# Score runs at three more steps of a fused attention and feed-forward kernel

## The chip, the core and the metric

One core of one Trainium2 chip. The metric is the device time of one execution in microseconds (us). TensorE (PE) multiplies, VectorE (DVE), ScalarE (ACT) and GpSimd (POOL) work on tiles, SyncE (SP) issues most transfers; each engine works its own list in order.

## The reference, cut to what matters

```python
batch, n_heads, seq, head_dim = (4, 8, 768, 64)      # 16 clusters
q_assign = np.argmax(np.einsum('bhsd,hcd->bhsc', q_n, c_n), axis=-1)
k_assign = np.argmax(np.einsum('bhsd,hcd->bhsc', k_n, c_n), axis=-1)
mask = q_assign[:, :, :, None] == k_assign[:, :, None, :]
scores = np.where(mask, scale * np.matmul(q, k.transpose(0, 1, 3, 2)), -1000000000.0)
attn = np.exp(scores - np.max(scores, axis=-1, keepdims=True))
attn = attn / (np.sum(attn, axis=-1, keepdims=True) + 1e-09)
x = np.matmul(attn, v)                               # to (3072, 512)
...
h = x @ w_in                                         # (512, 2048)
return ((h - np.tanh(h)) @ w_out).astype(np.float32)
```

## The kernel before

The attention is cut into 96 **steps** `(n, half, s)`: `n` is one of 16 pairs of heads (four to a batch), `half` one half of its queries, `s` one third of its keys. A step makes scores (`begin`, PE line L544, tiles `sc`), takes their exponent (ACT, L566), keeps the pairs of equal cluster (`select`, four DVE instructions L576 that read `sc` and a `row` of cluster codes and write `e`; with these four the two `sc` tiles of the step are free), adds `e` up (POOL, L588 and L592) and multiplies with the values (`value`, PE L601, tiles `av`). There are buffers for the two `sc` tiles of one step and for the `e` of two steps: the scores of a step wait for the select of the step before, and a select waits for the `value` of two steps before. Steps 72 to 95 are the pairs 12 to 15.

While a batch's attention runs, the feed-forward part of the batch before it fills the rest of PE's time: up products (`pu`, L1012 and L1021) and then down products (`pd`, L1301), taken from a list `fill` in order; each has a weight, and step by step as many are taken as their share of the total weight asks. During steps 72 to 95 there are 56 up and 14 down products: the seven products `which` = 1, 2, 6, 7, 4, 5, 3 of Strassen's scheme, each for two blocks `j` = 0 and 1.

The scores contract over 64 rows (the trace's `64*128`), the values, and as a rule the products, over 128 (`128*64`): PE changes its shape on the way into and out of the scores. In a **run** (`runs(at)`) the scores of the next three steps are made in one piece, and the two groups of products between them are made in the `64*128` shape as well. A down product then fills two banks, which DVE adds with one instruction more. Runs stood at steps 50, 53, 56, 59, 62, 65, 68, 74, 77 and 80.

The third block of batch 2 is not multiplied in its turn but **set aside** (`set_aside`): for each of the seven products SP stores the left operand (`aside<-G`, 512 KB), DVE adds its two halves into a tile `u` (L1266), and SP stores that (`aside<-u`, 256 KB, L1269). There are two `u` tiles, so a third sum waits until the store of the first has landed. Such work collects in the list `behind` and is put into the program in the next step that neither is a run nor stands just in front of one:

```python
            if not run and not runs(at + 1):
                todo += behind
                behind.clear()
```

After step 95 the up products of batch 3 (`pu`) follow and then its down products, one level deeper (`pp`, L1519); the last group stores four quarter rows.

Of the kernel before, what the change touches and what calls it, by code (L numbers as in the profile page):

```python
# [58 lines left out]
def kernel(  # L59
# [10 lines left out]
    nc = tc.nc  # L70
# [13 lines left out]
    HCH = NCH // 2  # L84
# [95 lines left out]
    def fast():  # L180
# [275 lines left out]
        def summed(n: int, half: int):  # L456

            return n < HP and half == 0
# [204 lines left out]
        def joined(n: int):  # L663

            return n >= HP and not soon(n)
# [24 lines left out]
        def soon(n: int):  # L690
            return pairs[n][1] == HP - 1 or n == HP - 2
# [154 lines left out]
        HM = DM // 2  # L846
        HQ, HC = HF // 2, HM // 2
# [7 lines left out]
        SET_ASIDE = {  # L855
            (0, 0): 1, (0, 1): 5, (1, 0): 2, (1, 1): 4, (2, 0): 7, (3, 0): 6, (5, 0): 3
        }
        behind = []
        aside = dram.tile([len(ASIDE), 7, P, HF + HQ, P], F32, name="aside", bufs=1)

        def up_maker(q: int):
# [343 lines left out]
        def strassen_items(b: int):  # L1205
# [31 lines left out]
            aside_ = sum(block[0] == b for block in ASIDE)  # L1237

            def weight(i: int):

                return 4.55 if aside_ else 3.4

            def lower(j: int, which: int, part: int):

# [5 lines left out]
                else:  # L1250
                    nc.gpsimd.tensor_tensor(out=a12, in0=a12, in1=a11, op=ALU.subtract)

            def set_aside(which: int):

                d = [i for i in range(len(ASIDE)) if ASIDE[i][0] == b]
                for i in d:
                    c = slice(ASIDE[i][1] * P, (ASIDE[i][1] + 1) * P)
                    quarter_ = {
                        1: (0, 0), 2: (1, 0), 3: (1, 0), 4: (1, 1), 6: (0, 0), 7: (0, 1)
                    }.get(which)  # L1260
                    t = G[:, :, quarter_[0], quarter_[1], c] if quarter_ else left1[:, :, c]
                    nc.sync.dma_start(aside[i, SLOT[which], :, 0:HF], t)
                    total_ = late_pools["u"].tile([P, 2, TB], F32, name="u")
                    total_ = total_.rearrange("p a n -> p (a n)")[:, 0 : HQ * P]
                    total_ = total_.rearrange("p (a n) -> p a n", n=P)
                    nc.vector.tensor_tensor(  # L1266
                        out=total_, in0=t[:, 0:HQ], in1=t[:, HQ:HF], op=ALU.add
                    )
                    behind.append(lambda total_=total_, i=i: nc.sync.dma_start(  # L1269
                        aside[i, SLOT[which], :, HF : HF + HQ], total_  # L1270
                    ))

# [221 lines left out]
            def group(at: int):  # L1494
# [9 lines left out]
                quarters = m.rearrange("p (a n) -> p a n", n=HC)  # L1504
# [27 lines left out]
                def row(half: int, m_: int, j: int):  # L1532
                    return out_r[blocks[j][0], half * HCH + blocks[j][1]][:, m_ * HM : (m_ + 1) * HM]
# [24 lines left out]
                )  # L1558
                if final:
                    add(m, m, u0)  # L1560
                    nc.sync.dma_start(row(0, 1, 0)[:, 0:HC], quarters[:, 0])
                    nc.sync.dma_start(row(0, 1, 1)[:, HC:HM], quarters[:, 3])
                yield
                pair = bank()
                if final:
# [92 lines left out]
            if b == B - 1:  # L1658
                n = len(ups)
# [23 lines left out]
        NS = NCH // 2  # L1683
        HALF = HP * NS
# [161 lines left out]

        def runs(at: int):

            return 4 * HALF < at < 7 * HALF - 1 and at % NS == NS - 1 and at % (2 * HALF) < 2 * HALF - 1

        fill, whole, spent, since, over = [], 0.0, 0.0, 0, 1
        for at, (n, half, s) in enumerate(steps):
# [11 lines left out]
            now = []  # L1864
# [5 lines left out]

            run, chunks = runs(at), []
            if run:
                coming = now + fill
                for _ in range(NS - 1):
                    size = 1 if coming[0][1] == 2 else 3
                    assert all(len(it) == 4 for it in coming[:size]) or size == 1
                    chunks.append(coming[:size])
                    coming = coming[size:]  # L1880
                first_ones = sum(len(it) for it in chunks)
                while len(now) < first_ones + 1:
                    now.append(fill.pop(0))
                    spent += now[-1][0]
                now = now[first_ones:]
            elif runs(at + 1):
                ups_left = sum(len(it) == 4 for it in fill)
                if ups_left < 3 * (NS - 1):
                    for _ in range(ups_left % 3):
                        now.append(fill.pop(0))  # L1890
                        spent += now[-1][0]
            values_first = 1 in stages and not summed(n, half) or run
            if values_first:
                value(n, half, s)
            if 1 in stages:
# [9 lines left out]
                        spread(*to[:2])  # L1905
            if run:
                take(n, half)
                if half == 1 and joined(n):
                    total_both(n)
                for i, it in enumerate(chunks):  # L1910
                    to = steps[at + 1 + i]
# [83 lines left out]
            todo = []  # L1995
            if not run:
                todo, held = held, []
# [3 lines left out]
            if following and not run:  # L2001

                if half == 1 and s == NS - 1 and joined(n):
                    todo.insert(len(todo) - 1, lambda n=n: total_both(n))
            if LOAD in stages:
                stages[LOAD]()
            if TURN_Q in stages:
# [49 lines left out]
            if 2 * HALF <= at < 3 * HALF:  # L2057
                masks = 3 if half == 1 and s == NS - 1 else 2
                first_masks, todo = todo[:masks], todo[masks:]
# [238 lines left out]
    with ExitStack() as cx, tc.manual_schedule():  # L2298
        fast()
# [34 lines left out]
```

## Time and profile before

| what | value |
|---|---|
| median of 3 runs | 923.16 us (922.49 to 923.47) |
| profiled execution, its own time | 922.68 us |
| its span | 920.8 us |
| PE busy | 908.1 us |
| mean granted PE clock | 0.999 |

The span is from the first to the last instruction that the profiler saw; 1.9 us of the execution lie around it. "Busy" is time with at least one instruction in an engine.

### The profile page before, as it was taken

What the parts mean: (1) busy time and instruction counts of PE and PEld (TensorE: products, weight loads), DVE (VectorE), ACT (ScalarE), POOL (GpSimd) and SP (SyncE); (2) the same over time, 40 slices, a digit from 0 to 9 for tenths busy, and PEclk for the clock granted to TensorE, in tenths of its full rate; (3) what the DMA queues carried; (4) which work ended last, traced back from release to release, by engine and by line L of the source; (5) the groups of instructions that cost most, each with busy time, mean ns of one, the idle gap of its engine ahead of it and who ended that gap; (6) DMA issues with size and microseconds to landing.
All of it is one profiled execution on the core that took longest, in us unless ns stands there. A gap on an engine that the chain in (4) does not pass through costs nothing.

```text
span 920.8 us, 18740 instructions
## 1 busy us (share of the span) xinstructions
PE 908.1 (99%) x7286; PEld 498.5 (54%) x7286; DVE 692.9 (75%) x1280; ACT 295.2 (32%) x466; POOL 523.6 (57%) x403
## 2 busy tenths in 40 slices
PE   8999999999999999999999999999999999999997
PEld 4434433356653454445666664555455554449997
DVE  7779777887799598667477477767697587867995
ACT  5676653234333233333321121343231311221000
POOL 0236433467878565977765565787776866772000
PEclk9999999999999999999999999999999999999999
DMA  8777583794428985375584746566546745524532
GB/s 168 226 221 180 155 194 105 229 266 141 107 86 224 272 261 141 120 189 175 159 191 151 186 143 169 177 179 161 178 150 205 230 156 155 189 103 151 196 105 85
DMA packets 187439, 158.37 MB, mean 172 GB/s; under 512 B 119200, under 2 KB 161744, under 8 KB 184144
## 3 DMA queue, kind: packets, MB, share of 16 engines
q1 hardware_dynamic: 177696, 134.40, 51.9%
q0 software_dynamic: 6048, 20.98, 6.9%
q10 hardware_dynamic: 3600, 1.74, 0.7%
q8 instruction: 59, 0.97, 0.4%
q14 instruction: 36, 0.29, 0.1%
HBM read 130.33 MB, written 26.75 MB: 171 GB/s over the span
## 4 chain that ended last, share of the span: by engine, by line
PE 92%; DVE 4%; ACT 1%; issue 1%; DMA 1%; POOL 0%; SPq 0%; DVEq 0%; ACTq 0%
PE pu L1021 20%; PE sc L544 15%; PE av L601 14%; PE pd L1301 12%; PE pp L1519 9%; PE o L803 6%; PE pu L1012 5%; PE h L787 5%; PE hd L1152 3%; PE sim L405 1%; DVE e L576 1%; PE den L674 1%; PE den L647 1%; PE den L627 1%; POOL G L1215 0%
## 5 line engine op out<-in xcount | busy, mean ns | idle before, releaser
L592 POOL TENSOR_TENSOR sum<-sum,e 128x768 f32<-128x768 f32 x112 | 206.5, 1844 | 78.7 <-DVE e L576 73.9
L576 DVE SCALAR_TENSOR_TENSOR e<-row,code,sc 128x384 f32<-128x384 bf16 x336 | 184.0, 608 | 56.7 <-ACT sc L566 31.6
L566 ACT ACTIVATE sc<-sc 128x768 f32<-128x768 f32 x168 | 126.4, 793 | 203.0 <-PE sc L544 182.4
L544 PE MATMUL sc<-t,t 64*128 64x384 f32 x768 | 149.1, 505 | 1.6 <-DVE e L576 1.1
L601 PE MATMUL av<-e,vals 128*64 128x384 f32 x768 | 143.4, 495 | 0.0
L1021 PE MATMUL pu<-xT,w_in 128*64 128x384 f32 (+1 forms) x872 | 132.5, 441 | 0.2 <-DVE c L1317 0.2
L1215 POOL TENSOR_TENSOR G<-G,th 128x768 f32<-128x768 f32 (+1 forms) x51 | 88.1, 1745 | 58.1 <-ACT th L1213 58.0
L1301 PE MATMUL pd<-w_in,G 128*64 128x256 f32 (+1 forms) x960 | 108.8, 379 | 0.0
L544 PEld LDWEIGHTS sc<-t,t 64*128 64x128 f32 x768 | 67.8, 186 | 70.5 <-issue 32.7
L1021 PEld LDWEIGHTS pu<-xT,w_in 128*64 128x64 f32 x872 | 61.6, 137 | 62.2 <-issue 50.2
L1301 PEld LDWEIGHTS pd<-w_in,G 128*64 128x64 f32 (+1 forms) x960 | 74.0, 147 | 35.6 <-issue 6.3
L601 PEld LDWEIGHTS av<-e,vals 128*64 128x64 f32 x768 | 49.7, 136 | 77.3 <-issue 73.5
L588 POOL TENSOR_TENSOR sum<-e 128x768 f32<-128x768 f32 x28 | 52.4, 1872 | 60.4 <-DVE e L576 46.4
L1021 PE MATMUL pu<-diff,w_in 128*64 128x384 f32 x416 | 74.1, 488 | 0.5 <-DVE u L1006 0.4
L1213 ACT ACTIVATE th<-G 128x768 f32<-128x768 f32 (+1 forms) x51 | 39.5, 806 | 107.8 <-DVE G L1006 90.9
L803 PE MATMUL o<-w_out,g 128*64 128x512 f32 x256 | 57.4, 593 | 0.0
L1021 PEld LDWEIGHTS pu<-diff,w_in 128*64 128x64 f32 x416 | 29.3, 137 | 37.9 <-issue 31.5
L1006 DVE TENSOR_TENSOR G<-pu,u 128x384 f32<-128x384 f32 x72 | 38.8, 550 | 13.5 <-PE pu L1021 12.1
L1012 PE MATMUL pu<-diff,w_in 64*128 64x384 f32 x160 | 45.8, 482 | 0.0
L1012 PE MATMUL pu<-xT,w_in 64*128 64x384 f32 x152 | 45.1, 482 | 0.0
L787 PE MATMUL h<-xT,w_in 128*64 128x384 f32 x256 | 42.8, 486 | 0.0
L638 ACT COPY xT<-av 128x384 f32<-128x384 f32 x32 | 15.3, 480 | 82.1 <-PE av L601 82.0
(283 smaller groups left out, 1286.0 us busy)
## 6 DMA issues: line engine op xcount, KB each, us to landing
w_in<-up_factors SPq DMA_DIRECT2D x32, 896.0 KB
w_in<-down_factors SPq DMA_DIRECT2D x25, 1024.0 KB
again<-in_moe_w_in_dram SPq DMA_DIRECT2D x32, 256.0 KB
again<-in_moe_w_out_dram SPq DMA_DIRECT2D x32, 256.0 KB
vals<-in_v_dram SPq DMA_DIRECT2D x32, 192.0 KB
raw<-in_moe_w_in_dram POOLq DMA_DIRECT2D x12, 512.0 KB, 4.8
row<-q_codes SPq DMA_DIRECT2D x29, 192.0 KB
raw<-in_moe_w_out_dram POOLq DMA_DIRECT2D x10, 512.0 KB, 4.8
```

The source lines that it names most:

```text
L544: nc.tensor.matmul(sc[i][:, h, 0:TB], lhsT=turned[n, 1][r].rearrange("p a n -> p (a n)")[:, j * P : (j + 1) * P], rhs=turned[n, 0][r, half ...
L566: nc.scalar.activation(out=out, in_=sc[i][:, :, 0:TB], func=ACT.Exp, scale=SCALE)
L576: nc.vector.scalar_tensor_tensor(out=e[:, h].rearrange("p (j n) -> p j n", n=P), in0=rows[n, half][:, h], scalar=(codes[n][:, h, 1, j : j ...
L592: nc.gpsimd.tensor_tensor(out=s, in0=s, in1=pair[i], op=ALU.add)
L601: nc.tensor.matmul(avs[n, half][h * D : h * D + D], lhsT=vals[n][:, h, j], rhs=e[i][:, h], start=(j == 0), stop=(j == NCH - 1),)
L787: nc.tensor.matmul(h[r], lhsT=w_in[i][:, c, o * P : (o + 1) * P][:, r], rhs=xT[c][:, half], start=(c == 0), stop=(c == CD - 1),)
L803: nc.tensor.matmul(acc[sub][r], lhsT=gs[f % HF][:, f // HF, sub * P : (sub + 1) * P][:, r], rhs=w_out[f // FQ][:, f % FQ], start=(f == seq ...
L1012: return nc.tensor.matmul(ps, lhsT=streams[base + i][r, c, k_], rhs=right[c][r], start=start, stop=stop)
L1021: nc.tensor.matmul(ps[r], lhsT=streams[base + i][:, c, k_, r], rhs=right[c], start=(c == 0), stop=(c == CH - 1),)
L1215: nc.gpsimd.tensor_tensor(out=t, in0=t, in1=th, op=ALU.subtract)
L1301: nc.tensor.matmul(out_, lhsT=w, rhs=x, start=(i == 0), stop=(i == HF - 1))
L1519: nc.tensor.matmul(ps[r], lhsT=left[:, i, r], rhs=right[i], start=(i == 0), stop=(i == HQ - 1),)
```

## The change

1. Runs also at steps 83, 86 and 89. At 86 and 89 (`before_`) one down product is put in front of `value`, and `total_both`, which sums the denominators, behind the run.
2. The weights of the 14 down products of batch 2 become a list, which sets in which step each stands.
3. The stores of the `u` tiles collect in `stores` and are issued at the next `set_aside`, or in the next piece of `behind`.
4. Two of the last four stores are issued by ACT in place of SP.

```diff
             def weight(i: int):
-                return 4.55 if aside_ else 3.4
+                if not aside_:
+                    return 3.4
+                i = i // HCH * (HCH - aside_) + i % HCH
+                return (3.4, 3.4, 8, 3.4, 3.4, 3.4, 14.2, 3.4, 3.4, 7, 7, 6, 2.7, 2.7)[i]
...
+            def store_sums():
+                while stores:
+                    stores.pop(0)()
+
             def set_aside(which: int):
+                store_sums()
+                behind.append(store_sums)
...
-                    behind.append(lambda total_=total_, i=i: nc.sync.dma_start(
+                    stores.append(lambda total_=total_, i=i: nc.sync.dma_start(
                         aside[i, SLOT[which], :, HF : HF + HQ], total_
                     ))
...
                 if final:
                     add(m, m, u0)
-                    nc.sync.dma_start(row(0, 1, 0)[:, 0:HC], quarters[:, 0])
-                    nc.sync.dma_start(row(0, 1, 1)[:, HC:HM], quarters[:, 3])
+                    nc.scalar.dma_start(row(0, 1, 0)[:, 0:HC], quarters[:, 0])
+                    nc.scalar.dma_start(row(0, 1, 1)[:, HC:HM], quarters[:, 3])
...
         def runs(at: int):
-            return 4 * HALF < at < 7 * HALF - 1 and at % NS == NS - 1 and at % (2 * HALF) < 2 * HALF - 1
+            return 4 * HALF < at < 8 * HALF - 4 and at % NS == NS - 1 and at % (2 * HALF) < 2 * HALF - 1
...
-            run, chunks = runs(at), []
+            run, chunks, before_ = runs(at), [], False
             if run:
                 coming = now + fill
+                before_ = at > 7 * HALF
+                if before_:
+                    first_, coming = coming[0], coming[1:]
...
-                first_ones = sum(len(it) for it in chunks)
-                while len(now) < first_ones + 1:
+                first_ones = sum(len(it) for it in chunks) + before_
+                while len(now) < first_ones + (not before_):
...
+            if before_:
+                first_[2](lambda: None)
             if values_first:
                 value(n, half, s)
...
-                if half == 1 and joined(n):
+                if half == 1 and joined(n) and not before_:
                     total_both(n)
...
+            if before_ and half == 1 and joined(n):
+                todo.append(lambda n=n: total_both(n))
```

PE, before, from the scores of step 87 to the product behind the values of step 89 (a row without a step's number: each `sc` is one step, each `av x4` the values of the step before it):

```order
L544 MATMUL sc<-t_5265,t_5249 128x384 x4
L601 MATMUL av<-e,vals 64x384 x4
L1301 MATMUL pd<-w_in_136,G 64x256 x16
L544 MATMUL sc<-t_5265,t_5249 128x384 x4
L601 MATMUL av<-e,vals 64x384 x4
L1301 MATMUL pd<-w_in_136,G 64x256 x16
L544 MATMUL sc<-t_5265,t_5249 128x384 x4
L601 MATMUL av<-e,vals 64x384 x4
L1301 MATMUL pd<-w_in_138,G 64x256 x16
L544 MATMUL sc<-t_5686,t_5678 128x384 x4
```

PE now, from the scores of step 87 to the product in the middle of the run at step 89 (L1310 is the old L1301; `128x256` are products in the shape of the scores):

```order
L544 MATMUL sc<-t_5276,t_5258 128x384 x4
L1310 MATMUL pd<-w_in_138,G 128x256 x16
L544 MATMUL sc<-t_5276,t_5258 128x384 x4
L1310 MATMUL pd<-w_in_138,G 128x256 x16
L544 MATMUL sc<-t_5276,t_5258 128x384 x4
L601 MATMUL av<-e,vals 64x384 x8
L1310 MATMUL pd<-w_in_137,G 64x256 x16
L601 MATMUL av<-e,vals 64x384 x4
L544 MATMUL sc<-t_5743,t_5719 128x384 x4
L1310 MATMUL pd<-w_in_137,G 128x256 x16
L544 MATMUL sc<-t_5743,t_5719 128x384 x4
```

The scores of steps 87, 88 and 89 and then of 90, 91 and 92 now stand in one piece each, and the values of 87 and 88 stand together.

DVE, before, from the second half of the select of step 88 to that of step 89: one sum for the block set aside (L1266) lies between.

```order
L576 SCALAR_TENSOR_TENSOR e_6017<-row_5792,code_5492,sc_5990 128x384 [waits Activation_49]
L576 SCALAR_TENSOR_TENSOR e_6017<-row_5792,code_5492,sc_5990 128x384
L475 CAST listed_codes_73<-code_5914 128x12 [waits DVE_49]
L477 STREAM_TRANSPOSE qc_6025<-listed_codes_73 128x32 [waits DVE_49]
L1317 SCALAR_TENSOR_TENSOR c_6031<-pd_6000,w_in3_139 128x256 [waits DMASW7_49,PE_49]
L1266 TENSOR_TENSOR u_6037<-G_3124 128x512 [waits DMAHW7_49]
L1776 TENSOR_REDUCE largest_69<-again_5983 128x1 [waits DMAHW4_49]
L1776 TENSOR_REDUCE largest_69<-again_5985 128x1 [waits DMAHW5_49]
L576 SCALAR_TENSOR_TENSOR e_6073<-row_5792,code_5492,sc_6043 128x384 [waits Activation_49,Pool_49]
```

DVE now, from the second instruction behind the select of step 89 (the cast L475 is the first) to the beginning of that of step 90 (`DMAHWn` are eight counters that SP's transfers use in turn: 5 in front of the second sum is that of the store of `u_5904`, 7 in front of the third that of `u_6087`, 5 in front of the select that of the load of `row_6105`):

```order
L477 STREAM_TRANSPOSE qc_6081<-listed_codes_73 128x32 [waits DVE_49]
L1275 TENSOR_TENSOR u_6087<-G_3124 128x512 [waits DMAHW2_49]
L1275 TENSOR_TENSOR u_6091<-G_3124 128x512 [waits DMAHW5_49]
L1275 TENSOR_TENSOR u_6096<-G_3124 128x512 [waits DMAHW7_49,DVE_49]
L1785 TENSOR_REDUCE largest_69<-again_5831 128x1 [waits DMAHW3_49]
L1785 TENSOR_REDUCE largest_69<-again_5833 128x1
L749 TENSOR_TENSOR xT_5523<-xT_5523,den_5755 128x384 [waits DMAHW1_49,DMAHW0_49]
L749 TENSOR_TENSOR xT_5523<-xT_5523,den_6063 128x384 [waits DMAHW3_49,DMAHW2_49]
L1326 SCALAR_TENSOR_TENSOR w_in3_139<-pd_6114,w_in3_139 128x256 [waits PE_49]
L1785 TENSOR_REDUCE largest_69<-again_6101 128x1 [waits DMAHW3_49]
L1785 TENSOR_REDUCE largest_69<-again_6103 128x1 [waits DMAHW4_49]
L576 SCALAR_TENSOR_TENSOR e_6152<-row_6105,code_5951,sc_6138 128x384 [waits DMAHW5_49,Activation_49,Pool_49]
```

Three sums, of the products 2, 4 and 7, have come together in front of the select of step 90; before, the second and the third stood behind later selects.

SP's queue, before, behind the cast and the transposition (L1269 and L1262 store the sums and the left operands, `row_6041` is for the select of step 90):

```order
L479 DMA q_codes_6027<-qc_6025 4x32x32 [waits DMAHW6_49,DVE_49]
L1269 DMA aside_150<-u_5966 128x512 [waits DMAHW7_49]
L1269 DMA aside_150<-u_5969 128x512 [waits DMAHW0_49]
L1262 DMA aside_150<-G_3124 128x8x128 [waits DMAHW1_49]
L499 DMA row_6041<-q_codes_6027 128x768 [waits DMAHW6_49,DMAHW2_49]
```

SP's queue now, over the same stretch (L1278 and L1271 store the sums and the left operands, `again` are loads for the two reduces, `row` is the load that the select of step 90 needs):

```order
L479 DMA q_codes_6083<-qc_6081 4x32x32 [waits DMAHW4_49,DVE_49]
L1278 DMA aside_150<-u_5904 128x512 [waits DMAHW5_49]
L1271 DMA aside_150<-G_3124 128x8x128
L1278 DMA aside_150<-u_6087 128x512 [waits DMAHW7_49,DVE_49]
L1271 DMA aside_150<-G_3124 128x8x128 [waits DMAHW0_49]
L1278 DMA aside_150<-u_6091 128x512 [waits DMAHW1_49,DVE_49]
L1271 DMA aside_150<-G_3124 128x8x128 [waits DMAHW2_49,Pool_49]
L1773 DMA again_6101<-in_q_dram 128x384 [waits DMAHW3_49,DVE_49]
L1773 DMA again_6103<-in_q_dram 128x384 [waits DMAHW4_49,DVE_49]
L499 DMA row_6105<-q_codes_6083 128x768 [waits DMAHW5_49]
```

The load of `row_6105` stands behind the two loads of `again`, which wait for the two reduces on DVE, which stand behind the three sums. Before, the load of that row was issued between the first pair of stores and the sum of product 2.

## Rows read from the trace of the kernel before

**Rows 1.** The page, busy time of each engine.

```profile
PE 908.1 (99%) x7286; PEld 498.5 (54%) x7286; DVE 692.9 (75%) x1280; ACT 295.2 (32%) x466; POOL 523.6 (57%) x403
```

**Rows 2.** Timeline of PE (start us, us, what), scores of steps 87 and 88.

```profile
681.46 1.56 PE L544 MATMUL sc<-t,t 64*128 64x384 f32 x8
682.95 1.51 PE L601 MATMUL av<-e,vals 128*64 128x384 f32 x8
...
687.85 1.56 PE L544 MATMUL sc<-t,t 64*128 64x384 f32 x8
```

**Rows 3.** Timeline of PE, one run with down products.

```profile
523.03 1.56 PE L544 MATMUL sc<-t,t 64*128 64x384 f32 x8
524.43 3.62 PE L1301 MATMUL pd<-w_in,G 64*128 64x256 f32 x32
527.88 1.46 PE L544 MATMUL sc<-t,t 64*128 64x384 f32 x8
529.17 3.62 PE L1301 MATMUL pd<-w_in,S 64*128 64x256 f32 x32
...
534.01 3.67 PE L1301 MATMUL pd<-w_in,S 128*64 128x256 f32 x32
```

**Rows 4.** Timeline of PE, three places with waits.

```profile
670.06 0.92 PE L544 MATMUL sc<-t,t 64*128 64x384 f32 x4
...
672.17 1.51 PE L601 MATMUL av<-e,vals 128*64 128x384 f32 x8
...
695.72 1.51 PE L601 MATMUL av<-e,vals 128*64 128x384 f32 x8
...
701.45 1.97 PE L544 MATMUL sc<-t,t 64*128 64x384 f32 x8 [0.77 <-DVE e L576]
703.35 1.51 PE L601 MATMUL av<-e,vals 128*64 128x384 f32 x8
...
753.94 2.75 PE L1021 MATMUL pu<-xT,w_in 128*64 128x384 f32 x16
756.94 2.80 PE L1021 MATMUL pu<-xT,w_in 128*64 128x384 f32 x16 [0.25 <-DVE c L1317]
759.88 1.51 PE L1021 MATMUL pu<-diff,w_in 128*64 128x384 f32 x8
```

**Rows 5.** Timeline of DVE around the sum of product 2.

```profile
691.86 2.04 DVE L475 CAST listed_codes<-code 128x12 bf16<-128x12 f32 x1
...
697.05 2.28 DVE L1266 TENSOR_TENSOR u<-G 128x512 f32<-128x512 f32 x1 [2.28 <-DMA aside<-u]
...
700.18 2.17 DVE L576 SCALAR_TENSOR_TENSOR e<-row,code,sc 128x384 f32<-128x384 bf16 x4
```

**Rows 6.** Timeline of SP's queue (issues) over the same stretch.

```profile
694.80 0.93 SPq L1269 DMA_DIRECT2D aside<-u  x2
...
696.34 0.65 SPq L499 DMA_DIRECT2D row<-q_codes  x1
```

**Rows 7.** Windows of 1 us: each engine's busy time, PEclk, DMA share, GB/s.

```profile
696.00:697.00 1.00, 1.00 (x8) 0.43 (x6) 0.00 (x0) 0.74 (x2) 0.98 (x2) 1.00 1.03 342
```

**Rows 8.** Two DVE lines: ns of one, min/median/max.

```profile
L1266 DVE TENSOR_TENSOR u<-G x6: 684/1540/2284, 685.5 to 746.2; 128x512 f32<-128x512 f32 x6
...
L749 DVE TENSOR_TENSOR xT<-xT,den x10: 543/627/2174, 495.1 to 749.8; 128x384 f32<-128x384 f32 x10
```

**Rows 9.** DVE's waits, whole span: total us, times, longest.

```profile
DVE e L576 <- DMA row<-q_codes: 6.4, 4, 2.3
```

**Rows 10.** Timeline of SP's and ACT's queues, last stores.

```profile
914.04 0.33 SPq L1561 DMA_DIRECT2D out_dram<-again  x1
...
914.94 0.36 ACTq L1572 DMA_DIRECT2D out_dram<-again  x1
```

**Rows 11.** A window after the last matmul, columns as in rows 7.

```profile
919.50:920.00 0.50, 0.00 (x0) 0.00 (x0) 0.00 (x0) 0.00 (x0) 0.00 (x0) 0.81 0.04 16
```

More of the change, by code (lines that the diff above doesn't have):

```diff
@@ L857, in fast @@
         }
-        behind = []
+        behind, stores = [], []
         aside = dram.tile([len(ASIDE), 7, P, HF + HQ, P], F32, name="aside", bufs=1)
```

## The prediction

> **What bounds the kernel now.** I read the page first: PE is busy for 908.1 us [rows 1], so a change counts by what it takes from PE's own list or by a wait that it puts into it. Then the timeline of PE from step 84 on, for the gaps between starts; then DVE's and SP's timelines at the places where PE waited. The reader is to see three things. In [rows 2] a step outside a run costs PE 687.85 - 681.46 = 6.39 us. In [rows 3] the same work inside a run costs less: 529.17 - 527.88 = 1.29 for the scores, 527.88 - 524.43 = 3.45 for a product. And in [rows 4] PE three times starts late because DVE is late.
>
> **What the change takes away.** The order lists show the same matmuls, in part in another shape.
>
> *Changes of shape.* Scores, values (eight matmuls of 384 columns like the scores, so 1.29) and a product take 1.29 + 1.29 + 3.45 = 6.03; the 6.39 of [rows 2] hold 0.36 for going into the scores' shape and out. A run pays that once for three steps (0.21 of it is seen inside one: 534.01 - 523.03 = 10.98 [rows 3] against 3 x 1.29 + 2 x 3.45 = 10.77). Nine groups of scores become three, six round trips fewer: 6 x 0.36 = **-2.2**. In the other shape a down product needs one more DVE addition; [rows 3] show that PE loses nothing by it there.
>
> *Waits.* From the scores at 670.06 to the values 2.11 passed [rows 4], against 1.49 in [rows 2]: 0.62. From values to scores 701.45 - 695.72 = 5.73 against 4.90 in [rows 2], and from there to 703.35 1.90 against 1.49: 1.24 together. The two pairs of up products from 753.94 take 3.00 and 2.94 where four groups like the scores would take 2.58 each: 0.78. All three sit in steps 84 to 95 or just behind, where DVE's list is now another one; behind step 95 two down products now stand between the last denominators and the up products, before only one. I take all away: **-2.6**; the bounds are 0 and -2.6.
>
> **What it adds: the sums set aside.** This is the large term. Before, the sum of product 2 alone delayed a select: the cast began at 691.86, the sum at 697.05 (it had waited 2.28 for the store of an older `u`), and the select of step 89 started at 700.18 [rows 5]; the scores behind it lost the 1.24 above. Now the sums of products 2, 4 and 7 stand together between the selects of 89 and 90, with two `u` tiles, and the row for step 90 is loaded behind them. I follow it with zero at the scores of step 87.
>
> PE: the run's scores and two products take 10.98 [rows 3]; values of 87 until 12.3, of 88 until 13.6, a product until 17.1, values of 89 until 18.4, then 0.1 for the change of shape, scores of 90 until 19.8, product until 23.3. At **23.3** PE wants the scores of 91, which need the first half of the select of 90.
>
> DVE: the select of 89 needs the `e` that the values of 87 free, so it runs from 12.3 to 14.5 (2.17, [rows 5]). Cast, transposition, store of the codes and the store of the waiting `u` follow each other as in [rows 5], with the store issued at 694.80 [rows 6]: 2.94 from cast to issue, 5.19 until the buffer was free. So the store is issued at 17.4 and the second sum begins at 19.7; the first lies in the gap. A sum takes 0.68 to 2.28, median 1.54 [rows 8]: until 21.2. The third needs the store of the first, issued some 0.95 later (two issues, [rows 6]) and behind 512 KB: 17.4 + 0.95 + 2.25, and 1.5 for 512 KB at the 342 GB/s of [rows 7], is 22.1. It ends at 23.6. The two reduces take 0.9 (between the end of the sum and 700.18 in [rows 5]) until 24.5; only then can the second `again` be loaded and, 0.5 later, the row: issued at 25.0. In [rows 5, 6] the row was there 3.84 after its issue (696.34 to 700.18; no wait for it is seen): 28.8. The two scalings (0.63 each, at most 2.17 [rows 8]), one addition and two reduces fit in beside it. First half of the select, half of 2.17: 29.9. **PE waits 29.9 - 23.3 = 6.6.** The second tile comes later still, as at 701.45: +0.4.
>
> Bounds: with sums of 0.68, no time for the 512 KB and a row that lands in the 2.25 of a `u` store, the third sum ends at 21.3, the row is there at 24.9 and PE waits 2.7. With sums of 2.28 and a row load 2.3 later (the longest that a select has waited for one, [rows 9]) it is 24.4, 25.8, 31.9, 33.0: 9.7. I stay in the middle, since each link has a row of its own.
>
> A sum alone takes 0.68, yet the median is 1.54 and the one in [rows 5] took 2.28 while POOL was busy in almost every moment [rows 7]. The Trainium skill, "SBUF — State Buffer", section "SBUF: two separate sides", says that a DVE instruction with two SBUF inputs and a GpSimd instruction that reads SBUF lock each other out for a whole instruction. By that rule each of the three sums, with POOL adding `e` beside them, is a long one, and the wait would be nearer to 8 than to 6.6; the trace agrees with the rule for single sums.
>
> **Smaller terms.** The scores of step 93 now follow the values of 90 and 91 without a product between, and the select of 92 starts only with the end of the values of 90: its second half is over 2.2 after that, the scores ask for it after 1.29 + 0.1 + 0.65. With releases **+0.3** (0 to 1). The fourth of ACT's stores: before, SP's first left at 914.04 and ACT's last at 914.94 [rows 10]; four in one queue, 0.36 and a little each, put the last near 915.2, and all ends with its landing: **+0.25** (0 to 0.3). The first product in front of the values in steps 86 and 89 costs nothing: it is work that would stand elsewhere, and it covers the select that those values need. The denominators behind the run move two PE groups and four small transfers to a place where three steps pass before anyone needs them. The new weights move products, and with them the loads of their factors, which still have a product or more in hand.
>
> **Sum:** -2.2 - 2.6 + 6.6 + 0.4 + 0.3 + 0.25 = +2.75, on the profiled execution's own 922.68: 925.4. The median of the runs is 0.5 above that execution; I say **925.6 us**. Bounds of the long wait alone: 921.5 to 928.5.
>
> **Rivals.**
> - *PE does not wait for step 90* (the other side). Speaking for it: the first sum, and without locks all of DVE's own work between the selects (2.0 + 0.2 + 3 x 0.68 + 0.9 + 1.3 + 0.4 + 0.9 = 7.7), ends at 22.2, and stores might land faster than the one seen. Then only the gains are left: 922.68 - 2.2 - 2.6 + 0.55 = 918.4. It decides at a select of 90 that begins before 22.2. Against it: two transfers that DVE waits for in turn, each 2.25 in the only row there is.
> - *The clock falls during the wait.* The granted clock was still full until 919.5 and then fell [rows 11], some 5 us after the last matmul. If a wait of 6.6 lets it fall to 1.2 GHz, the next product takes twice 3.45: 925.6 + 3.5 = 929. No row shows a matmul at that clock, so the price may be smaller.
> - *The runs do not do what they are for:* outside the older runs the round trip costs nothing extra, or moves to the values, which now stand in pairs. Without the 2.2 it is 927.8. Against it: [rows 2, 3] show the same groups side by side.
>
> **How the numbers follow.** About 0.2% (1.85 us) is what a measurement of this kernel can tell from no change. Long wait as priced, 0.58 (0.30 of it over +1.85, 0.25 within, 0.03 faster); no wait, 0.22; clock falls, 0.15; runs without gain, 0.05. So faster 0.03 + 0.22 = 0.25, same 0.25, slower 0.30 + 0.15 + 0.05 = 0.50. The range, 920.0 to 930.0, takes in the bounds of the wait and the clock, and leaves out most of the case without a wait. The likeliest case's own range is 921.5 to 928.5.
>
> **What would show it.** Right: a gap of 3 to 10 us on PE in front of the second scores of the run at step 89, released by DVE's select; the third sum waiting for `aside<-u`, and the select of step 90 for `row<-q_codes`; three groups of scores with products of 3.45 between them in place of nine single ones. Wrong: scores of step 91 on time, or the three old waits still there. The prediction fails if the stores land within some 1.5 us of their issue, or if the select of step 89 ends well before 14.5.

## The result: 1.2% slower

| | kernel before | changed kernel |
|---|---|---|
| median, 6 runs each | 923.32 us (922.49 to 925.32) | 934.38 us (932.69 to 936.53) |
| ratio, 95% interval | | 1.012 (1.0103 to 1.0137) |
| profiled execution, its span | 922.68, 920.8 | 936.09, 934.2 |
| mean granted PE clock | 0.999 | 0.991 |

The time lies above the range of the prediction. I account for the two profiled executions, which differ by 13.4 us.

The page of the changed kernel, busy time; PE does the 7286 matmuls of [rows 1] in 2.6 us more, within a span 13.4 longer, so most of the difference is waiting:

```profile
PE 910.7 (97%) x7286; PEld 507.7 (54%) x7286; DVE 692.8 (74%) x1285; ACT 295.0 (32%) x466; POOL 524.0 (56%) x403
```

PE's timeline of the changed kernel, from the scores of step 87 to the first up products of batch 3:

```profile
690.40 1.56 PE L544 MATMUL sc<-t,t 64*128 64x384 f32 x8
...
701.38 2.80 PE L601 MATMUL av<-e,vals 128*64 128x384 f32 x16
...
708.85 1.56 PE L544 MATMUL sc<-t,t 64*128 64x384 f32 x8
710.25 2.11 PE L1310 MATMUL pd<-w_in,G 64*128 64x256 f32 x18
...
722.41 2.93 PE L544 MATMUL sc<-t,t 64*128 64x384 f32 x8 [8.55 <-DVE e L576]
725.11 4.51 PE L1310 MATMUL pd<-w_in,G 64*128 64x256 f32 x32
729.44 1.47 PE L544 MATMUL sc<-t,t 64*128 64x384 f32 x8
...
734.89 1.97 PE L544 MATMUL sc<-t,t 64*128 64x384 f32 x8 [0.48 <-DVE e L576]
736.79 1.51 PE L601 MATMUL av<-e,vals 128*64 128x384 f32 x8
738.13 3.62 PE L1310 MATMUL pd<-w_in,G 128*64 128x256 f32 x32
744.31 1.55 PE L647 MATMUL den<-sum,ones 128*64 128x384 f32 x4 [2.55 <-POOL sum L592]
745.78 2.31 PE L544 MATMUL sc<-t,t 64*128 64x384 f32 x8
748.03 1.51 PE L601 MATMUL av<-e,vals 128*64 128x384 f32 x8
...
760.97 0.87 PE L647 MATMUL den<-sum,ones 128*64 128x384 f32 x4 [0.30 <-POOL sum L592]
...
768.57 5.33 PE L1021 MATMUL pu<-xT,w_in 128*64 128x384 f32 x32
```

The run itself works: 701.38 - 690.40 = 10.98, to the hundredth the run of [rows 3], and from the scores of step 87 to those of step 90 pass 708.85 - 690.40 = 18.45, against 3 x 6.39 = 19.17 for three steps outside a run [rows 2]. Then come two waits. The scores of step 91 were wanted at 710.25 + 3.45 = 713.70 and start 8.71 later. The denominators of step 93 (L647) were wanted at 741.58 and start 2.73 later, released by POOL. Behind both, the same matmuls take longer: the scores at 722.41 need 2.70 to the next start, against 1.29 in [rows 3].

Windows of the changed kernel over these waits, columns as in [rows 7] (the number after the five engines is PEclk):

```profile
713.70:718.00 4.30, 0.17 (x2) 0.00 (x0) 2.43 (x6) 0.00 (x0) 0.00 (x0) 0.84 0.96 275
718.00:722.40 4.40, 0.00 (x0) 0.02 (x1) 1.52 (x4) 0.00 (x0) 0.00 (x0) 0.50 0.76 241
723.50:725.00 1.50, 1.50 (x6) 0.98 (x6) 0.57 (x2) 0.80 (x1) 0.00 (x0) 0.50 1.04 429
744.30:746.00 1.70, 1.69 (x6) 0.51 (x8) 0.00 (x0) 0.10 (x1) 1.70 (x2) 0.50 0.83 202
```

The clock fell to 0.50 (1.2 of 2.4 GHz) while PE waited and was still there when PE worked again.

DVE's timeline, the chain of the prediction:

```profile
706.34 2.25 DVE L1275 TENSOR_TENSOR u<-G 128x512 f32<-128x512 f32 x1
709.35 0.92 DVE L1275 TENSOR_TENSOR u<-G 128x512 f32<-128x512 f32 x1 [0.76 <-DMA aside<-u]
712.04 1.12 DVE L1275 TENSOR_TENSOR u<-G 128x512 f32<-128x512 f32 x1 [1.78 <-DMA aside<-u]
713.09 1.00 DVE L1785 TENSOR_REDUCE largest<-again 128x1 f32<-128x384 f32 x2
...
717.23 1.02 DVE L1785 TENSOR_REDUCE largest<-again 128x1 f32<-128x384 f32 x2 [1.87 <-DMA again<-in_q_dram]
721.13 2.19 DVE L576 SCALAR_TENSOR_TENSOR e<-row,code,sc 128x384 f32<-128x384 bf16 x4 [2.88 <-DMA row<-q_codes]
...
733.61 2.19 DVE L576 SCALAR_TENSOR_TENSOR e<-row,code,sc 128x384 f32<-128x384 bf16 x4 [3.02 <-POOL sum L588]
```

SP's queue:

```profile
715.27 0.44 SPq L499 DMA_DIRECT2D row<-q_codes  x1
```

POOL's timeline:

```profile
731.77 1.81 POOL L588 TENSOR_TENSOR sum<-e 128x768 f32<-128x768 f32 x1 [19.15 <-PE den L674]
```

The row was issued 24.87 after the scores of step 87 (predicted 25.0) and landed 5.86 later, when the select that waited for it started (predicted 3.84). The second wait was not in the prediction: POOL's sum of step 90 needs a `sum` tile. There are two, and until the denominators of pair 14 (L674, now behind the run, at 730.84) both hold that pair's sums. The select of step 90 was done at 723.3; POOL started at 731.77 and was late for everything after.

### The profile page after: what moved, and what is told of

Read it like the earlier page. It is cut to its first block, busy times and chain, and to the rows that moved or that the text cites. A ratio compares the mean times of both kernels' runs of the same rounds, so it can differ in the third digit from the quotient of the medians.

```text
span 934.2 us, 18747 instructions
## 1 busy us (share of the span) xinstructions
PE 910.7 (97%) x7286; PEld 507.7 (54%) x7286; DVE 692.8 (74%) x1285; ACT 295.0 (32%) x466; POOL 524.0 (56%) x403
## 4 chain that ended last, share of the span: by engine, by line
PE 83%; DVE 5%; DMA 5%; POOL 3%; issue 2%; ACT 1%; SPq 1%; ACTq 0%; DVEq 0%; POOLq 0%
PE pu L1021 20%; PE sc L544 12%; PE pd L1310 11%; PE av L601 11%; PE pp L1528 9%; PE pu L1012 6%; PE h L787 4%; PE hd L1152 3%; PE o L803 3%; DVE e L576 1%; DMA row<-q_codes 1%; PE sim L405 1%; POOL sum L592 1%; DMA hot<-q_codes 1%; DMA q_codes<-qc 1%
## 5 line engine op out<-in xcount | busy, mean ns | idle before, releaser
L1021 PE MATMUL pu<-xT,w_in 128*64 128x384 f32 (+1 forms) x864 | 130.3, 440 | 0.0
L1310 PE MATMUL pd<-w_in,G 128*64 128x256 f32 (+1 forms) x960 | 109.6, 381 | 0.0
L1310 PEld LDWEIGHTS pd<-w_in,G 128*64 128x64 f32 (+1 forms) x960 | 79.4, 157 | 31.4 <-issue 5.4
L1021 PE MATMUL pu<-diff,w_in 128*64 128x384 f32 x400 | 71.4, 488 | 0.4 <-DVE u L1006 0.4
L1012 PE MATMUL pu<-diff,w_in 64*128 64x384 f32 x176 | 49.6, 482 | 0.0
L1012 PE MATMUL pu<-xT,w_in 64*128 64x384 f32 x160 | 48.3, 482 | 0.0
```

Of the source, the lines that this page charges most:

```text
L1012: return nc.tensor.matmul(ps, lhsT=streams[base + i][r, c, k_], rhs=right[c][r], start=start, stop=stop)
L1021: nc.tensor.matmul(ps[r], lhsT=streams[base + i][:, c, k_, r], rhs=right[c], start=(c == 0), stop=(c == CH - 1),)
L1310: nc.tensor.matmul(out_, lhsT=w, rhs=x, start=(i == 0), stop=(i == HF - 1))
```

## Experiments

The names A, B, V, L, R, W are those of the expectations. Experiments 1 to 7 and 9 to 12 are edits of the changed kernel; 8 is one of the kernel before.

**1. Denominators in front of the run again.**

```diff
-                if half == 1 and joined(n) and not before_:
+                if half == 1 and joined(n):
                     total_both(n)
...
-            if before_ and half == 1 and joined(n):
-                todo.append(lambda n=n: total_both(n))
```

> The changed kernel with the denominators of pair 14 (L674) in front of the run of step 89 again; all else stays. Theory A (the denominators behind the run hold both `sum` tiles, so POOL's sum of step 90 starts 8 us late and its backlog makes PE wait again at 734.9, 744.3 and 761.0, with a low clock at 744 to 748): those three places, worth 0.59 + 0.41 + 2.73 + 0.72 + 0.76 + 0.47 = 5.7 us, are gone, POOL's L588 waits for `e` instead of for `den`, the long wait of 8.7 in front of the scores of step 91 stays: about 928.7. Rival B (POOL is late because the select of step 90 is late, whatever the tile): the second wait stays at 2 us or more and the time at 933 or more.

Measured: 930.28 us, ratio to before 1.0076 (1.0059 to 1.0092). POOL's waits from 700 to 740 (total, times, longest):

```profile
POOL sum L588 <- DVE e L576: 10.7, 1, 10.7
```

POOL now waits for `e`, the wait of 2.73 is gone, and 4.1 us with it. A holds, B falls. Not all that A lists belongs to the denominators: a wait of 0.34 in front of the last denominators stayed, and so did 0.68 at the scores of step 93 (0.27 late, 0.41 longer). The first wait is 7.7 because the denominators fill 0.78 of it.

**2. The row's load in front of the two loads of `again`.**

```diff
                 todo += behind
                 behind.clear()
+                if at == 7 * HALF + 3:
+                    todo.append(lambda: spread(n + 1, 0))
...
-                if to and to[2] == 0 and kind == known:
+                if to and to[2] == 0 and kind == known and at != 7 * HALF + 4:
```

> The changed kernel with the load of the row for step 90 issued right behind the three left operands and sums, in front of the two loads of `again`. Theory A (the row is late because its issue stands behind loads that wait for two reduces, which stand behind three sums): it is issued at about 711.6 in place of 715.27, the select of step 90 waits for DVE's own reduces and starts near 718.4 in place of 721.13, the wait in front of the scores of step 91 falls from 8.7 to about 6.0, the second wait stays: about 931.7. Rival B (the row lands when the stores of 512 KB are through, whenever it is issued): select at 721, no change, 934.4.

Measured: 935.57 us, ratio 1.0132 (1.0115 to 1.0149): nothing gained. SP's queue and DVE's timeline:

```profile
711.45 1.22 SPq L499 DMA_DIRECT2D row<-q_codes  x1
712.72 1.71 SPq L1773 DMA_DIRECT2D again<-in_q_dram  x2
```

```profile
719.17 1.05 DVE L1785 TENSOR_REDUCE largest<-again 128x1 f32<-128x384 f32 x2 [4.75 <-DMA again<-in_q_dram]
720.14 2.18 DVE L576 SCALAR_TENSOR_TENSOR e<-row,code,sc 128x384 f32<-128x384 bf16 x4
```

The row is issued early, but the select of step 90 now starts directly behind the two reduces, whose loads stand behind the row and landed at 719.2, over 6 us after their issue. A's number falls, the time is B's. When the row itself landed, this run does not show.

**3. Edits 1 and 2, and the reduces and loads of `again` of step 87 later.**

```diff
-                if not run and not runs(at + 1) and at != 7 * HALF:
+                if not run and not runs(at + 1) and at not in (7 * HALF, 7 * HALF + 3):
                     todo += [check_done, check_done, check_on, check_on]
```

> Both edits above, and the reduces and loads of `again` of step 87 moved to later steps. Theory A: the three sums end at 713.2, the select starts when the two additions and two older reduces are done or the row has landed, 716.6 to 717.5; the first wait is 3.4 to 4.3 in place of 8.7, the waits behind it are gone: 934.4 - 5.7 - 4.8 = about 923.9, or 921.6 if the clock no longer falls. Rival B (the place of the row and of the denominators are not the cause): above 930.

Measured: 931.15 us, ratio 1.0083 (1.0066 to 1.0100). The row is issued at 711.49; DVE has nothing else left and waits for it:

```profile
718.87 2.19 DVE L576 SCALAR_TENSOR_TENSOR e<-row,code,sc 128x384 f32<-128x384 bf16 x4 [4.40 <-DMA row<-q_codes]
```

7.4 us from issue to landing; and the last denominators wait 1.6 for POOL. So the place behind the reduces was not what made the row late. The time is that of rival B, though the denominators do cost something (experiment 1). Both 2 and 3 missed my numbers for one reason: I counted a fixed time from a load's issue to its landing, while SP's transfers of 706 to 712 were still on their way in front of it.

**4. Experiment 3, and the sum of product 7 behind the run.**

```diff
-            (0, 0): 1, (0, 1): 5, (1, 0): 2, (1, 1): 4, (2, 0): 7, (3, 0): 6, (5, 0): 3
+            (0, 0): 1, (0, 1): 5, (1, 0): 2, (1, 1): 4, (3, 1): 7, (3, 0): 6, (5, 0): 3
```

> The third kernel, and in it the sum of product 7 is collected two products later, so that it falls behind the run of step 89 and only the sums of products 2 and 4 stand in front of the select of step 90. Theory A (the chain of sums and stores is the rest of the wait): the sums end at 710.3, the select starts at 713.8 to 715.5, PE wants the scores of step 91 at 714.5 and waits 0.4 to 2.3; no second wait, no low clock: about 919, below the kernel before. Rival B (two sums behind the run make the next selects late instead): a wait of 2 to 4 us in front of the scores of step 93 or 94, about 922.

Measured: 930.94 us, ratio 1.0102 (1.0068 to 1.0136). With 0.75 MB less in front, the select of step 90 still waits for the row, issued at 710.06, until 717.08; PE's wait there is 3.8. A wait of 1.97 came up in front of the scores of step 94, where B had put one of 2 to 4. Both numbers are missed, and the sum itself was not the rest of the wait.

**5. The row in front of all stores.** Experiment 3, but the row right behind the codes; the older `u` stored before the run; product 7 later still (`(4, 1): 7`).

```diff
-            yield lambda: publish(n)
+            yield lambda: (publish(n), spread(n, 0) if n == len(pairs) - 1 else None)
...
                     first_, coming = coming[0], coming[1:]
+                    while stores:
+                        stores.pop(0)()
```

> The first kernel (denominators in front), and: the row for step 90 is loaded right behind the store of the codes, in front of all the stores for the block set aside; the store of the older `u` leaves before the run; the sum of product 7 is collected later; the reduces of step 87 come later. Theory V (volume: the row lands when the 2 to 3 MB of stores and loads that stand in the queue in front of it are through, at some 300 GB/s): with nothing in front it is issued near 709 and lands within 4 us, the select of step 90 starts by 713.5, PE wants the scores of step 91 at 714.5 and waits under 0.5: about 920.6. Theory L (latency: a row load takes its 6 to 7 us wherever it stands): the select starts at 715.5, the wait is about 2 and the clock falls behind it: about 924.

Measured: 927.35 us, ratio 1.0035 (1.0023 to 1.0046). DVE's and PE's timelines:

```profile
710.18 3.15 DVE L749 TENSOR_TENSOR xT<-xT,den 128x384 f32<-128x384 f32 x2
...
714.51 2.18 DVE L576 SCALAR_TENSOR_TENSOR e<-row,code,sc 128x384 f32<-128x384 bf16 x4
```

```profile
713.72 5.19 PE L1310 MATMUL pd<-w_in,G 64*128 64x256 f32 x29 [2.12 <-DVE w_in L1326]
```

The select no longer waits for the row, and the wait of 8 us is gone. When the row landed is not seen, only that it was there 6.1 after its issue at 708.41, so this run does not decide between V and L; experiment 10 does. Two other waits came up, and the time misses both numbers: a down product waits 2.12 for a PSUM bank that DVE frees only behind two additions (L749), and the last denominators wait 2.24 for POOL.

**6. Experiment 3 with the three left operands stored behind the run.**

```diff
-                    nc.sync.dma_start(aside[i, SLOT[which], :, 0:HF], t)
+                    keep_ = lambda i=i, t=t: nc.sync.dma_start(aside[i, SLOT[which], :, 0:HF], t)
+                    if which in (2, 4, 7):
+                        lefts_.append(keep_)
+                    else:
+                        keep_()
```

`lefts_` is issued with the first `behind` after step 89.

> The third kernel (denominators in front, row early, reduces later) with the stores of the three left operands, 512 KB each, moved behind the run; the three sums, their stores and the row's place stay. Theory V (volume): the row, issued near 711, lands within 4 us, the select of step 90 starts at 714.5 to 715 in place of 718.87 (shifted by at most 0.7 between executions), and the wait in front of the scores of step 91 falls from 6.4 to 1.5 to 2.5: about 925. Theory L (latency): the row lands 6 to 7 after its issue as in the third kernel, select at 717.5 or later, no gain, 931.

Measured: 932.67 us, ratio 1.0106 (1.0072 to 1.0141). The row, issued at 711.08, landed at 716.69, 5.6 later: between V and L. The first wait fell from 6.4 to 2.97, but the 1.5 MB, now in front of the load of `each` (the denominators, of which L714 takes the reciprocal), brought a new one of 5.45 in front of the scores of step 94.

**7. Without the run at step 89.**

```diff
-            return 4 * HALF < at < 8 * HALF - 4 and ...
+            return 4 * HALF < at < 7 * HALF + 4 and ...
```

> The changed kernel without the run at step 89; the runs at 83 and 86, the weights and the three sums together stay. Theory A (the three sums, the stores and the row load behind them are the first wait; the denominators behind the run the second): the first wait stays at 5 us or more, there is no second: 927 to 930. Rival R (the run at step 89, which asks for the scores of 91 after one product, is what makes the select late): no wait over 2 us in steps 90 and 91, and 923 or less.

Measured: 931.17 us, ratio 1.0079 (1.0060 to 1.0097). PE's timeline:

```profile
720.26 2.93 PE L544 MATMUL sc<-t,t 64*128 64x384 f32 x8 [8.03 <-DVE e L576]
```

The wait does not need the run at 89: what collects behind the run at 86 is enough. A holds, R falls, though the time is 1 above A's numbers.

**8. Only the last stores by ACT** (the fourth part of the change, on the kernel before).

> The kernel before with nothing but the fourth part of the change: two of the last four stores by ACT. The term of the prediction: +0.25 us from the last addition to the end of the span (6.19 in the kernel before). What the changed kernel's profile showed: 5.81, so -0.4. In the time neither can be told from no change: 923 to 924.

Measured: 924.05 us, ratio 1.0004 (0.9990 to 1.0018). The last addition starts at 915.80, the span ends at 922.2: 6.4, against 6.19 in the kernel before and 5.81 in the changed one. My -0.4 was an accident of one execution; the term is not to be told from nothing.

**9. The run at 83 alone.**

```diff
-            return 4 * HALF < at < 8 * HALF - 4 and ...
+            return 4 * HALF < at < 7 * HALF and ...
```

> The changed kernel with the run at step 83 alone; the weights and the stores stay. Theory A (the losses come from the sums that collect because of the runs at 86 and 89): the sums stand one by one between the selects again, no wait over 1.5 us in steps 84 to 95, two round trips of 0.36 and the wait of 0.62 at step 86 saved: 922 to 923. Rival W (the new weights, which move the products, are part of the loss): 926 or more.

Measured: 923.03 us, ratio 0.9990 (0.9977 to 1.0003). PE's waits:

```profile
PE sc L544 <- DVE e L576: 1.1, 2, 0.7
```

A holds, W falls: with the new weights and one new run, but no collecting, nothing is lost that the times could show. PE waits 0.33 for POOL in front of the last denominators, as in experiment 1. The gain that the rows promise is too small to be told from no change.

**10. Experiment 5, with product 7 behind step 94 (`(5, 1): 7`) and L749 behind the run.**

```diff
-                    scaled = 7 if n >= 2 * HP and p == 0 else 5
+                    scaled = 7 if n >= 2 * HP and p == 0 or n == 3 * HP + 1 else 5
```

> The fifth kernel with the sum of product 7 collected still later, behind step 94, and the two additions to `xT` of pair 13 (L749) moved from in front of the select of step 90 to behind the run. If the remaining cost of the fifth kernel is what its profile shows, 2.1 for the bank that DVE frees behind these additions, 1.8 and 0.7 for the low clock behind that wait, and 1.5 of the 2.2 in front of the last denominators, it takes about 921.3, below the kernel before by 2 to 3. If another wait takes their place, 924 or more.

Measured: 925.25 us, ratio 1.0013 (1.0002 to 1.0024). SP's queue, then DVE's and PE's timelines:

```profile
706.77 0.32 SPq L499 DMA_DIRECT2D row<-q_codes  x1
```

```profile
710.41 2.19 DVE L576 SCALAR_TENSOR_TENSOR e<-row,code,sc 128x384 f32<-128x384 bf16 x4 [0.54 <-DMA row<-q_codes]
...
725.29 3.72 DVE L749 TENSOR_TENSOR xT<-xT,den 128x384 f32<-128x384 f32 x2
...
730.78 0.23 DVE L714 RECIPROCAL each<-each 128x12 f32<-128x12 f32 x1 [0.84 <-DMA each<-list]
730.92 2.15 DVE L576 SCALAR_TENSOR_TENSOR e<-row,code,sc 128x384 f32<-128x384 bf16 x4
```

```profile
712.84 1.46 PE L544 MATMUL sc<-t,t 64*128 64x384 f32 x8
...
732.17 2.93 PE L544 MATMUL sc<-t,t 64*128 64x384 f32 x8 [2.59 <-DVE e L576]
```

With no transfer of SP but 8 KB of codes in the 2 us in front of it, the row lands 3.64 after its issue, as V says and L does not; the scores of step 91 are on time, and all of the run of step 89 is free of waits. But the select of step 93 now stands behind L749 and L714: the second outcome that I named, another wait.

**11. Experiment 10, with L749 and L714 behind the select of step 93.**

```diff
+                    scaled = 9 if n == 3 * HP + 1 else 7 if n >= 2 * HP and p == 0 else 5
...
+                    more = more or n == 3 * HP + 2
                     for i, stage in (
```

> The kernel with everything moved (the tenth), in which the select of step 93 stood behind the two additions L749 and behind L714, which waits for `each`: now both come behind that select. If what its profile showed is all, the 2.6 in front of the scores of step 94 and the 1.5 of low clock behind it go: 925.25 - 4.1 = about 921.1, ratio to the kernel before 0.997. If the next transfer or buffer takes their place (the row of the second half, which the same select needs, or the bank behind L749), 923.5 or more.

Measured: 925.35 us, ratio 1.0015 (1.0002 to 1.0027). The row of the second half, issued at 722.47 behind 1 MB of factors, landed 8.81 later and took the place, the second outcome that I named:

```profile
731.28 2.19 DVE L576 SCALAR_TENSOR_TENSOR e<-row,code,sc 128x384 f32<-128x384 bf16 x4 [3.42 <-DMA row<-q_codes]
```

The wait in front of the scores of step 94 fell to 1.41, but the last denominators now wait 2.54 for POOL.

**12. Without the run at step 86 (runs at 83 and 89), denominators in front.**

```diff
-            return 4 * HALF < at < 8 * HALF - 4 and ...
+            return 4 * HALF < at < 8 * HALF - 4 and at != 7 * HALF + 2 and ...
```

> The changed kernel without the run at step 86, with the runs at 83 and 89, and with the denominators in front of the run at 89. The steps 84 to 87 are free for the sums again, so they need not collect, and the row for step 90 stands behind one left operand and one `u`. Theory A (the collecting of the sums, which the run at 86 brings about, is the cause; a run by itself gains 0.7): no wait over 2 us in front of the scores of step 91, 922 to 923. Rival R (a run at step 89 asks too early for the scores of 91 in any case): a wait of 4 us or more there, 926 or more.

Measured: 928.68 us, ratio 1.0040 (1.0027 to 1.0054). PE's and DVE's timelines:

```profile
717.07 1.46 PE L544 MATMUL sc<-t,t 64*128 64x384 f32 x8
...
737.47 2.89 PE L544 MATMUL sc<-t,t 64*128 64x384 f32 x8 [3.81 <-DVE e L576]
```

```profile
732.69 1.75 DVE L1275 TENSOR_TENSOR u<-G 128x512 f32<-128x512 f32 x1 [4.19 <-POOL G L1252]
736.10 0.23 DVE L714 RECIPROCAL each<-each 128x12 f32<-128x12 f32 x1 [1.66 <-DMA each<-list]
```

The scores of step 91 are on time, so a run at 89 does not by itself make them late: R falls there. The time missed A's number all the same, since what collects behind the run at 89 (two sums, one of which waits for POOL, and then L714, which waits for `each`) delays the select of step 93.

## Why the prediction was wrong

| term, by the prediction's own steps | predicted | in the profile after |
|---|---|---|
| changes of shape | -2.2 | -2.2, what is left over of this account (0.72 of it is seen in steps 87 to 89) |
| old waits | -2.6 | -2.6: all three gone |
| long wait for step 90 | +6.6 | +8.7 |
| its second tile, and scores of 93 | +0.7 | +1.0, all at step 93 (0.59 late, 0.41 longer; 0.68 in experiment 1) |
| denominators behind the run | 0 | +2.7 (at 744.31) |
| last denominators of the batch | none | +0.5 (at 760.97; as much in experiments 1 and 9, so not from the denominators behind the run) |
| low clock | a rival, +3.5 | +3.8 (1.41 and 0.88 at 722.41, 0.72 and 0.76 at 744.31) |
| last stores, and the rest of the end | +0.25 | -0.45 |
| in front of all that was changed | none | +2.0 |
| sum | +2.75 | +13.4 |

**The step that failed** is "The denominators behind the run move two PE groups and four small transfers to a place where three steps pass before anyone needs them", costed at nothing. I asked who needs what the denominators make, and not who needs the buffers that they read. Experiment 1 puts the price, with the low clock behind it, at 4.1 us. It is not the whole miss: without it the kernel still takes 930.28, by the two steps that follow.

**The long wait was right in place and cause, and too short by 2.1.** The chain came as written up to the row's issue, in part by luck: the reduces were done 23.7 after the scores of step 87 in place of 24.5, and the row left 1.2 behind them in place of 0.5. The term that was mis-sized is "the row was there 3.84 after its issue", and it was misread as well. The row issued at 696.34 is `row_6041`, for step 90; the select at 700.18 is that of step 89, which reads the older `row_5792`. The select of step 90 began at 706.29, behind other work of DVE, so the kernel before shows only that the row landed within 9.95:

```profile
706.29 1.13 DVE L576 SCALAR_TENSOR_TENSOR e<-row,code,sc 128x384 f32<-128x384 bf16 x2
```

That 3.84 is near the 3.64 of experiment 10 is luck. Behind other transfers of SP it was 5.86 here and 7.4 in experiment 3. I had put 512 KB in front of the third `u` at 342 GB/s, and forgot the same for the row. What the delay goes with is not all that was issued before the row, but what of it was still on its way. This is estimated from the sizes of SP's issues less what the windows show as moved by then:

| row | still on its way, estimate | issue to landing |
|---|---|---|
| experiment 10 | 0 MB | 3.64 us |
| experiment 6 | 0.3 MB | 5.61 us |
| changed kernel | 0.6 MB | 5.86 us |
| experiment 4 | 0.9 MB | 7.02 us |
| experiment 3 | 1.0 MB | 7.38 us |
| experiment 11, second half | 1.4 MB | 8.81 us |

The Trainium skill, "DMA: Bandwidth & Descriptors", section "Queues, rings and completion order", says that on each DMA engine the descriptors of one issuing engine are taken in the order of the ring; these rows agree with it. It does not explain all: at some 300 GB/s the 0.3 MB of experiment 6 are 1 us, and the row took 2 more than in experiment 10. What held it there stays open.

**The clock was a rival at 0.15, and it fell.** It should have stood in the sum, since both waits of the changed kernel were followed by matmuls at half the clock. My +3.5 was for the first wait alone, which cost 2.3; the second wait had its own 1.5.

**The rule on SBUF did not decide it.** Of the three sums one was long (2.25) and two short (0.92, 1.12), so the wait came near 8 by another way. Beside the second sum it was POOL that took longer (its two additions from 708.00 took 3.39, against 2.50 for the same two in the kernel before). Where POOL adds beside DVE, the rows agree with the rule: the two additions of L749 took 3.15 in experiment 5, with POOL busy until 712.9, and 1.01 in the changed kernel, with POOL idle.

**What was right:** the old waits went, the run gains what it should, the first product in front of the values costs nothing, the gap is where it was said to be.

**The 2.0 in front** arose before any changed instruction. The same scores, first of a run, start at these times in the kernel before, in experiment 8 (the same program up to the last stores) and in the changed kernel:

```profile
496.74 1.56 PE L544 MATMUL sc<-t,t 64*128 64x384 f32 x8
```

```profile
497.94 1.56 PE L544 MATMUL sc<-t,t 64*128 64x384 f32 x8
```

```profile
498.75 1.56 PE L544 MATMUL sc<-t,t 64*128 64x384 f32 x8
```

The first two differ by 1.2 with no change in front of them. In experiments 1, 9, 10 and 11, which are the changed kernel up to there, these scores start at 498.36, 498.05, 497.11 and 498.68, a spread of 1.6 with 498.75, so most of the 2.0 differs from one execution to the next (not all ran on one chip). The medians differ by 11.1 and the profiled executions by 13.4, because the changed kernel's profiled execution lies 1.7 above its median and the other 0.6 below; differences of this kind would do that, but no run shows it.

No version beat the kernel before by more than the measurement can tell. Experiments 10 and 11 have all three runs and stand within 0.2% of it, on the slow side. The 4.8 that runs and old waits give is spent again: 6.1 in experiment 10, on waits in steps 93 to 95 and the low clock behind one of them, and 5.4 in experiment 11, on such waits alone.

## What to carry to other kernels

A stretch that is packed tight for one engine is a stretch in which deferred work cannot go out; before packing it, list what collects in front of and behind it, and follow that work to the first instruction that waits for it. Of a step that is moved later, ask not only who needs its output but which buffers it keeps, and who writes them next. A load that the next step needs is to be timed from the bytes in front of it in its queue that are still on their way, and placed ahead of bulk stores, even if its issuing queue has to wait a little for it.

## What was not expected of the hardware

- The clock can fall after PE is at work again. In experiment 5 PE waited 2.1 us until 713.72; windows of its profile:

```profile
711.00:713.70 2.70, 0.61 (x4) 0.19 (x1) 2.70 (x4) 1.13 (x2) 1.92 (x2) 1.00 1.11 356
713.70:716.00 2.30, 2.28 (x18) 1.97 (x20) 2.30 (x5) 0.00 (x0) 0.00 (x0) 0.82 1.13 330
716.00:718.00 2.00, 2.00 (x12) 1.63 (x10) 0.69 (x2) 0.00 (x0) 1.17 (x1) 0.50 0.95 352
```

  Waits of like length differ: behind one of 2.59 (experiment 10) the scores took 2.86 to the next start at a clock of 0.50, behind one of 2.97 (experiment 6) 1.77 at a clock of 1.00, against 1.29 to 1.49 without a wait. A wait of 1.41 (experiment 11, scores of step 94) left the clock at 1.00 in the windows from 731.0 to 736.0.
- The same load, a row of 192 KB, landed 3.3 us (experiment 11, step 90) to 8.8 us (experiment 11, step 93) after its issue, the later the more of SP's earlier transfers was still on its way.
